# Softmax sums of short and last groups spread by VectorE instead of a DMA, longer planned DMA latencies, less forced filler

## The chip, the cores and the metric

One core of one Trainium2 chip. The metric is device time in microseconds (us), the median over executions. ACT is ScalarE, DVE is VectorE, PE is TensorE, POOL is GpSimd, SP is SyncE. One profile was taken of each kernel, so what is read from a profile carries the scatter of one execution; the slowest execution of a kernel in one series of runs lies 1 to 9 us above the fastest here.

## The reference, cut to what matters

```python
x = A_x                                    # [1, 2048, 512] bf16
x = x + _A_ref(_layernorm(x), A_wqkv, A_wo)
x = x + _B_ref(_layernorm(x), B_w1, B_w2)
x = x + _A_ref(_layernorm(x), A_wqkv, A_wo)
x = x + _B_ref(_layernorm(x), B_w1, B_w2)
# _A_ref: 32 heads of 16, softmax(q k^T / 4) v, then wo.   _B_ref: relu(h w1) w2, width 1792
```

Two layers, each attention and feed-forward. Attention has 2 x 32 x 2048 x 2048 exponentials. That is the work that matters; in this kernel ACT and DVE do it.

## The kernel before

The kernel plans its own order: while it is built, a small model with planned durations decides which instruction comes next on each engine. Each engine then runs its fixed order and waits on semaphores. A "slot" is one activation: three PSUM banks of scores (1536 columns). In about a quarter of the slots the third bank goes to DVE, which computes the exponential with integer and polynomial steps in pairs of banks, so ACT does 1024 columns. PE fills what is left of a slot with value matmuls, dense matmuls ("filler": projections and feed-forward) and, if nothing else fits, with repeated score matmuls, meant to keep its clock up.

The softmax sums of a group of 512 queries lie in one partition of each 32 of an accumulated tile `u`. To divide, the kernel gathers them into 128 partitions (`c`), takes the reciprocal, writes them back and spreads each row over 32 partitions (`r`) by a DMA:

```python
        def copy():
            ...                                        # u = sums and values out of PSUM
            if sg not in segs[-2:]:
                nc.sync.dma_start(out=c, in_=sums)     # the gather
                mark(("c", n), lag=3000.0)             # planned latency, ns
        def recip():
            nc.vector.reciprocal(out=c, in_=c)
            nc.sync.dma_start(out=sums, in_=c)         # the write-back
            nc.gpsimd.dma_start(out=r[:, 0:width], in_=...)   # the spread, [0, 32] repeated
            mark(("r", n), lag=9500.0)
        ...
            task(250, recip, [("r", n)], [("c", n)], place=0)
            task(180 + 1.1 * width, lambda: mul(0, width), ots + [("m", n)], [("r", n)] + war)
```

The last two groups of all take a shuffle on DVE instead, as nothing hides a DMA there. "Short groups" are those whose keys come in two or three parts; their partial sum is stored and loaded again (`sg["load"]`). Dense work is placed by pace, and is forced past the slot's limit when the pace is high:

```python
    def fill_pe(limit):
        while owed[0] > 0:
            limit_now = limit if owed[0] < 5.0 or not hurry[0] else now_pe[0] + 1000.0
            ...
        hurry[0] = pace > HURRY                        # HURRY = 2.0
    ...
    while pend:                                        # after the last slot
        emit_pv()
        run_dve(0.0, musts)
    run_all()                                          # whatever dense work is left, one PSUM bank
    wide[0] = True                                     # then the tail: last wo, layernorm, feed-forward
```

The softmax here doesn't subtract the row's maximum and nothing guards it: scores larger than these inputs give would overflow.

## Time and profile before

| Kernel before | us |
|---|---|
| median (3 runs) | 1757.56 (1755.46 to 1758.97) |
| span of the profiled execution | 1758.8 |
| start of the first exponential | 18.2 |
| end of the last exponential | 1726.5 |
| from there to the end ("the tail") | 32.3 |
| floor of ACT: slots by undisturbed start-to-start time | 1671.8 |
| loss: first start to last end, minus floor | 36.4 |

How to read it: three terms make the span. The prologue is load and layernorm; the tail is what must follow the last exponential; between them ACT sets the time, and what it does beyond its floor is a loss. How the floor is worked out from the start times of the activations, and why not from "idle", stands in the prediction, with the lines of the profile.

### The profile page before, as it was taken

How to read it: one execution, taken by the hardware profiler on the slowest of the kernel's cores; microseconds unless marked ns; L12 is line 12 of the kernel's file. 1: busy time of each engine (PE TensorE's matmuls, PEld its weight loads, DVE VectorE, ACT ScalarE, POOL GpSimd, SP SyncE). 2: the span in 40 equal slices, each digit the busy share in tenths (PEclk: the TensorE clock that was granted, in tenths of full speed). 3: DMA queues.
4: the chain of work that ended last, by engine and by line, in shares of the span. 5: the costliest groups of instructions: out<-in, count | busy, mean ns of one | idle time of the engine just before them, and what ended most of it. 6: DMA issues, size and time to landing. Idle time of an engine off the chain costs nothing.

```text
span 1758.8 us, 34642 instructions
## 1 busy us (share of the span) xinstructions
PE 1603.6 (91%) x14939; PEld 523.5 (30%) x15133; DVE 1482.0 (84%) x2221; ACT 1705.6 (97%) x1386; POOL 54.8 (3%) x105
## 2 busy tenths in 40 slices
PE   8898888999999999899899999879999999999998
PEld 2222222222222222222222222222222222444444
DVE  7438988888998999899789989879889888889884
ACT  6999999999999999999999999989999999999994
POOL 0000000000000000000000000000000000000000
PEclk9999999999999999999999999999999999999999
DMA  4001000110002000011000100010220021102112
GB/s 150 1 6 21 14 14 14 35 29 14 8 14 44 19 14 14 17 37 23 8 7 10 25 10 1 17 36 8 46 45 16 14 44 23 26 15 48 24 35 66
DMA packets 110937, 44.53 MB, mean 25 GB/s; under 512 B 98816, under 2 KB 106752, under 8 KB 110784
## 3 DMA queue, kind: packets, MB, share of 16 engines
q1 hardware_dynamic: 92192, 24.38, 6.0%
q0 software_dynamic: 17248, 16.63, 5.0%
q8 instruction: 118, 1.93, 0.4%
q10 hardware_dynamic: 1344, 1.31, 0.2%
q14 instruction: 35, 0.29, 0.1%
HBM read 22.54 MB, written 2.10 MB: 14 GB/s over the span
## 4 chain that ended last, share of the span: by engine, by line
ACT 84%; PE 11%; DVE 2%; issue 2%; DMA 1%; ACTq 0%
ACT e L1141 84%; PE ps_s L1132 4%; PE ps_o L823 3%; PE ps_f L409 2%; PE ps_s L1207 1%; DVE dy L900 0%; DMA c<-u 0%; DVE di L869 0%; DVE stats L438 0%; PE ps_f L1207 0%; PE ps_s L968 0%; DMA x<-in_A_x_dram 0%; DVE ht L622 0%; DVE q L570 0%; PE ps_s L477 0%
## 5 line engine op out<-in xcount | busy, mean ns | idle before, releaser
L1141 ACT ACTIVATE e<-ps_s 128x1536 bf16<-128x1536 f32 (+1 forms) x1366 | 1695.2, 1456 | 13.4 <-PE ps_s L1132 12.4
L1132 PE MATMUL ps_s<-q,ktp 32*128 32x512 bf16 (+1 forms) x7817 | 746.2, 357 | 118.6 <-ACT e L1141 91.3
L823 PE MATMUL ps_o<-e,vaug 128*32 128x512 bf16 (+1 forms) x4224 | 428.0, 363 | 4.7 <-DVE u L758 3.2
L1132 PEld LDWEIGHTS <-ktp 32*128 32x128 bf16 x7817 | 235.8, 92 | 619.3 <-issue 500.6
L869 DVE TENSOR_SCALAR di<-ps_s 128x512 int32<-128x512 f32 x338 | 232.3, 688 | 94.0 <-PE ps_s L1132 91.2
L823 PEld LDWEIGHTS <-vaug 128*32 128x32 bf16 x5376 | 144.9, 94 | 301.3 <-issue 277.6
L900 DVE SCALAR_TENSOR_TENSOR dy<-dm 128x1024 f32<-128x1024 f32 x169 | 206.4, 1221 | 3.8
L900 DVE SCALAR_TENSOR_TENSOR dy<-dy,dm 128x1024 f32<-128x1024 f32 x169 | 205.7, 1217 | 2.7
L900 DVE SCALAR_TENSOR_TENSOR de<-dy,di 128x1024 bf16<-128x1024 f32 x169 | 205.1, 1214 | 1.7
L894 DVE TENSOR_SCALAR dm<-di 128x1024 int32<-128x1024 int32 x169 | 116.6, 690 | 0.9
L823 PE MATMUL ps_o<-de,vaug 128*32 128x512 bf16 (+1 forms) x768 | 114.7, 358 | 2.2 <-DVE vaug L739 0.8
L894 DVE TENSOR_SCALAR di<-di 128x1024 int32<-128x1024 int32 x169 | 115.2, 681 | 1.7
L409 PE MATMUL ps_f<-xn2T,w 128*128 128x512 bf16 (+1 forms) x390 | 112.5, 368 | 4.4 <-issue 1.9
L409 PE MATMUL ps_f<-w,ht 128*128 128x512 bf16 x344 | 103.4, 383 | 4.5 <-issue 4.0
L783 POOL DMA_DIRECT2D r<-u x70 | 52.4, 748 | 1654.4 <-DMA u<-c 643.5
L622 DVE TENSOR_SCALAR ht<-ps_f 128x512 bf16<-128x512 f32 x105 | 72.1, 686 | 18.0 <-PE ps_f L409 15.9
L409 PE MATMUL ps_f<-xnT,wqkv 128*128 128x512 bf16 (+1 forms) x273 | 82.4, 372 | 3.4 <-issue 0.8
L570 DVE TENSOR_SCALAR q<-ps_f,qmask 128x512 bf16<-128x512 f32 (+1 forms) x94 | 63.1, 699 | 13.0 <-PE ps_f L409 11.4
L823 PE MATMUL ps_o<-di,vaug 128*32 128x512 bf16 (+1 forms) x384 | 70.9, 365 | 0.0
L409 PE MATMUL ps_f<-wo,ot 128*128 128x512 bf16 x207 | 63.5, 383 | 2.8 <-issue 2.2
L773 DVE SCALAR_TENSOR_TENSOR ot<-u,mask,r 128x512 bf16<-128x512 f32 (+2 forms) x74 | 49.8, 673 | 7.5 <-DMA r<-u 7.1
L409 PEld LDWEIGHTS <-w 128*128 128x128 bf16 x448 | 32.5, 97 | 73.1 <-issue 62.2
(85 smaller groups left out, 535.2 us busy)
## 6 DMA issues: line engine op xcount, KB each, us to landing
w<-in_B_w_dram SPq DMA_DIRECT2D x126, 128.0 KB
r<-u POOLq DMA_DIRECT2D x56, 256.0 KB, 7.1
out_dram<-x SPq DMA_DIRECT2D x16, 128.0 KB
x<-in_A_x_dram SPq DMA_DIRECT2D x14, 128.0 KB
w<-in_B_w_dram SPq DMA_DIRECT2D x1, 1792.0 KB
r<-u POOLq DMA_DIRECT2D x14, 128.0 KB, 4.6
wqkv<-in_A_wqkv_dram ACTq DMA_DIRECT2D x2, 512.0 KB
c<-u SPq DMA_DIRECT2D x56, 8.0 KB
```

The costliest lines, as they stand in the source:

```text
L409: nc.tensor.matmul(out, lhsT, rhs, start=i % k == 0, stop=i % k == k - 1)
L570: return nc.vector.tensor_scalar(out=qbuf[n % 2][e][:, 0:w], in0=b, scalar1=qmask[e][:, 0:1], scalar2=None, op0=ALU.mult,)
L622: nc.vector.tensor_scalar(out=htp[ft // 2][:, ft % 2 : ft % 2 + number, a : a + w], in0=b.rearrange("p (f q) -> p f q", f=number), scalar1 ...
L773: nc.vector.scalar_tensor_tensor(out=ot[t][:, at_column + a : at_column + a + w], in0=u[:, a : a + w], scalar=mask[e][:, 0:1], in1=r[:, a ...
L783: nc.gpsimd.dma_start(out=r[:, 0:width], in_=bass.AP(tensor=sums.tensor, offset=sums.offset, ap=[list(sums.ap[0]), [0, 32], [1, width]],),)
L823: nc.tensor.matmul(ps_o[32 * g : 32 * g + 32, 0 : sg["w"]], vaug[sg["l"]][kb][:, 4 * sg["T"] + g, 2 * e : 2 * e + 32], rhs, start=g not in ...
L869: first = nc.vector.tensor_scalar(out=di[:, half, :].bitcast(I32), in0=src, scalar1=EXP_BIAS, scalar2=0.0, op0=ALU.add, op1=ALU.max,)
L894: nc.vector.tensor_scalar(out=out[:].bitcast(I32), in0=di[:].bitcast(I32), scalar1=keep, scalar2=put, op0=ALU.bitwise_and, op1=ALU.bitwise_or,
L900: nc.vector.scalar_tensor_tensor(out=out[:], in0=x[:], scalar=c, in1=y[:], op0=ALU.add, op1=ALU.mult)
L1132: nc.tensor.matmul(b[:, a : a + sg["w"]], kt[32 * g : 32 * g + 32, kc : kc + P], qbuf[sg["n"] % 2][sg["e"]][32 * g : 32 * g + 32, 0 : sg[" ...
L1141: ex = nc.scalar.activation(out=eb[:, 0 : place[m]], in_=b[:, 0 : place[m]], func=ACTF.Exp, scale=1.0 / (LOG2E * UNIT),)
L1207: uses(nc.tensor.matmul(out, lhsT, rhs, start=first, stop=last), b, needs=needs)
```

## The change

The intent: no spread DMA where its latency stands in the way (short groups, last group of a chunk of queries); plan DMAs with the latency that they have, so that DVE does not block on one; and force less dense work between score matmuls, since that makes ACT wait.

```diff
-    HURRY = 2.0
+    C_LAG, R_LAG, U_LAG = 3600.0, 10500.0, 3000.0
...
+        quick = sg["load"] is not None or ended[l, j] == NT
...
         def recip():
             nc.vector.reciprocal(out=c, in_=c)
             nc.sync.dma_start(out=sums, in_=c)
-            nc.gpsimd.dma_start(
+            if not quick:
+                nc.gpsimd.dma_start(
...
-            mark(("r", n), lag=9500.0)
+            mark(("r", n), lag=U_LAG if quick else R_LAG)
+        def spread():
+            nc.vector.stream_shuffle(
+                out=r[:, 0:width], in_=u[:, 0:width], mask=[lane] * 32
+            )
+        def spread_mul():
+            if quick:
+                spread()
+            mul(0, width)
...
-            rest = sum(x[0][0]["early"] for x in itertools.islice(units, 400)) / W - 10.0
+            rest = sum(x[0][0]["early"] for x in itertools.islice(units, 400)) / W - 20.0
...
-        hurry[0] = pace > HURRY
+        hurry[0] = pace > (
+            2.0 if first["l"] and first["early"]
+            else 3.0 if not first["l"] and first["j"] == NQS - 1 else 99.0
+        )
```

Below, "the shuffle", "the lags" and "the filler rule" (the last two hunks) are its three parts.

More of the change, by code (lines that the diff above doesn't have):

```diff
@@ L765, in copy @@
                 nc.sync.dma_start(out=c, in_=sums)
-                mark(("c", n), lag=3000.0)
+                mark(("c", n), lag=C_LAG)
         musts.append((155 + 1.045 * width, now_pe[0] + PE_TO_DVE, copy))
@@ L778, in mul @@
                 mark(("ot", l, j, t, i))
+        ended[l, j] = ended.get((l, j), 0) + 1
+        quick = sg["load"] is not None or ended[l, j] == NT
         def recip():
@@ L782, in recip @@
             nc.sync.dma_start(out=sums, in_=c)
-            nc.gpsimd.dma_start(
-                out=r[:, 0:width],
-                in_=bass.AP(
-                    tensor=sums.tensor, offset=sums.offset,
-                    ap=[list(sums.ap[0]), [0, 32], [1, width]],
-                ),
-            )
-            mark(("r", n), lag=9500.0)
+            if not quick:
+                nc.gpsimd.dma_start(
+                    out=r[:, 0:width],
+                    in_=bass.AP(
+                        tensor=sums.tensor, offset=sums.offset,
+                        ap=[list(sums.ap[0]), [0, 32], [1, width]],
+                    ),
+                )
[3 more added lines that the diff above has]
+                out=r[:, 0:width], in_=u[:, 0:width], mask=[lane] * 32
+            )
+        def spread_mul():
+            if quick:
+                spread()
+            mul(0, width)
         def direct(i):
             if i == 0:
-                nc.vector.stream_shuffle(
-                    out=r[:, 0:width], in_=u[:, 0:width], mask=[lane] * 32
-                )
+                spread()
             a = i * P
@@ L811, in finish_segment @@
             task(250, recip, [("r", n)], [("c", n)], place=0)
-            task(180 + 1.1 * width, lambda: mul(0, width), ots + [("m", n)], [("r", n)] + war)
-        ended[l, j] = ended.get((l, j), 0) + 1
+            cost = 180 + 1.1 * width + (200 + 1.05 * width if quick else 0)
+            task(cost, spread_mul, ots + [("m", n)], [("r", n)] + war)
         if ended[l, j] == NT and not last:
```

## The prediction

> **What bounds the kernel now.** I read the page first (busy shares, chain), then the ScalarE (ACT) groups by shape, then the waits, then the timeline at two places where the chain leaves ACT.
>
> ```profile
> PE 1603.6 (91%) x14939; PEld 523.5 (30%) x15133; DVE 1482.0 (84%) x2221; ACT 1705.6 (97%) x1386; POOL 54.8 (3%) x105
> ...
> ACT 84%; PE 11%; DVE 2%; issue 2%; DMA 1%; ACTq 0%
> ```
>
> ACT is the bound: it computes the exponentials, and the chain that ended last is ACT for 84%. PE, 91% busy, is partly filler: score matmuls are repeated to keep it warm.
>
> ```profile
> L1141 ACT ACTIVATE e<-ps_s 128x1536 bf16<-128x1536 f32 x1027 | 1445.5, 1564 | 7.0 <-PE ps_s L1132 6.3
> L1141 ACT ACTIVATE e<-ps_s 128x1024 bf16<-128x1024 f32 x338 | 378.7, 1131 | 6.4 <-PE ps_s L1132 6.1
> ```
>
> Here the reader must not trust "idle": consecutive activations overlap, so a delay up to the overlap is counted as busy. I took start-to-start distances from the trace instead. Undisturbed, a 1536-wide one is followed after 1.330 us and a 1024-wide one (its third bank went to VectorE, DVE) after 0.903 us. 1027 x 1.330 + 338 x 0.903 + 0.68 for one 512-wide one = 1671.8 us. The stretch from the first start (18.2) to the last end (1726.5) is 1708.3 us. So the loop loses 36.4 us; 18.2 us of prologue and 32.3 us of tail make up the rest of the span.
>
> Where are the 36.4 us? Two kinds. First, waits on the DMAs that spread a group's softmax sums:
>
> ```profile
> ACT e L1141 <- PE ps_s L1132: 12.4, 28, 2.2
> ...
> DVE ot L773 <- DMA r<-u: 7.1, 9, 2.1
> ...
> DVE c L781 <- DMA c<-u: 4.6, 2, 3.3
> ```
>
> ```profile
> 1153.53 0.69 DVE L758 TENSOR_TENSOR u<-ktp,ps_o 128x512 f32<-128x512 f32 x1 [0.34 <-PE ps_o L823]
> ...
> 1160.57 0.25 DVE L781 RECIPROCAL c<-c 128x16 f32<-128x16 f32 x1 [3.30 <-DMA c<-u]
> ```
>
> ```profile
> 1165.00 1.02 ACT L1141 ACTIVATE e<-ps_s 128x1024 bf16<-128x1024 f32 x1 [2.17 <-PE ps_s L1132]
> 1166.58 1.45 ACT L1141 ACTIVATE e<-ps_s 128x1536 bf16<-128x1536 f32 x1 [0.55 <-PE ps_s L1132]
> ```
>
> Read downward: sums copied at 1153.5, DVE blocked for 3.30 us on the gather into c, all behind it late, ACT starved at 1165. Start-to-start, four slots from 1147 to 1167 lose 5.3 us. Three more delays with PE waiting for a late DVE copy lose 1.7 us, one at a clock drop (219 us) 1.4 us.
>
> Second, PE holding too much between two score groups ("forced filler"):
>
> ```profile
> 1256.96 1.02 ACT L1141 ACTIVATE e<-ps_s 128x1024 bf16<-128x1024 f32 x1 [0.18 <-PE ps_s L1132]
> 1258.36 1.02 ACT L1141 ACTIVATE e<-ps_s 128x1024 bf16<-128x1024 f32 x1 [0.37 <-PE ps_s L1132]
> ```
>
> 1.40 us from start to start instead of 0.90. In the program's order PE has there 5 value matmuls (1.67 passes, as three share the array), 2 dense and one score pass: 4.67 x 0.216 + 3 switches x 0.105 = 1.32 us against 0.90. I tallied every slot so: 32 are overloaded by over 0.3 us, and they lose 9.7 us. Small losses on the other slots make up the rest.
>
> **What the skill says.** "VectorE: DVE Perf Modes", section "The perf-mode tier table": the stream shuffle has only the 1x mode, about 2400 ns for 2048 elements. The trace agrees: its two shuffles of 256 took 438 ns, so a fixed 0.171 us beside 256/0.96 ns, and 512 elements should take 0.70 us (estimate). "DMA: Bandwidth & Descriptors", "Anatomy of one DMA — SWDGE (gpsimd) path" gives 2.0 us + bytes/436e3, 2.6 us for the 256 KB spread; the page's row for r<-u has 7.1 us to landing, and that decides. Same page, "Issuing engines are not separate DMA queues": all share 16 engines. This agrees with the gather from 1154: 6.0 us to its last packet against 1.5 usually, beside r transfers. "TensorE: Matmul & The Clock Gate", "What's actually happening": a window of 3413 ns with too little work halves PE's clock. The trace agrees: 3.4 us at 0.50 at 219.2, 1164.7 and 1738.1 us.
>
> **The change, part by part.**
>
> (a) Shuffle for the 20 groups with a carried partial sum and the last group of a chunk. The built programs give 70 spread DMAs before, 45 after; 2 shuffles before, 27 after (24 new of 512, one of 256). Removed per group: the wait from the written-back reciprocals to the landing, about 9.5 us from the reciprocal (2.4 to the issue, 7.1 in flight); left is a write-back of about 2 us and 0.70 us on DVE. DVE cost: 24 x 0.70 + 0.44 = 17.2 us. It saves the 5.3 us above and shortens chunk ends, where nothing waits visibly.
>
> (b) The longer lags (3.6 and 10.5 us planned for 3.0 and 9.5) let DVE's queue put other work first. They address the 11.7 us of DVE waits in the waits view; DVE is not the bound, so their worth is already in (a) and the small losses.
>
> (c) The built order has 166 DVE pairs instead of 169. A pair costs 2 x 0.688 + 1.221 + 1.217 + 1.214 + 0.690 + 0.681 = 6.40 us, so DVE gets 19.2 us back and stays even. ACT gets 6 banks more: 1033 x 1.330 + 332 x 0.903 + 0.68 = 1674.4, that is +2.6 us.
>
> (d) Less forced filler. The same tally on the new order: slots overloaded by over 0.3 us fall from 32 to 8. With the mean loss of each overload class from the trace (17 ns for slots with ample room, about 50 for mild ones, 350 for the worst) the old order gives 28.0 us and the new one 21.9. Saved: 6.1 us. Repeated score passes rise from 968 to 1033; they only fill holes.
>
> With (a) leaving perhaps 2 us of the 8.4 us DMA and late-copy losses, the loop loses 24 us instead of 36.4. With (c) its end comes 12.4 - 2.6 = 9.8 us earlier.
>
> (e) The price of (d), to be seen at the end of the order. The old order leaves half a feed-forward group of the last chunk but one (4 matmuls, one DVE evacuation) behind the last value matmuls; the new order leaves all seven (56 matmuls of 256 columns, 7 evacuations) there, through a single PSUM bank.
>
> ```profile
> 1725.47 1.42 PE L823 MATMUL ps_o<-e,vaug 128*32 128x256 bf16 x20
> ...
> 1726.83 0.61 PE L409 MATMUL ps_f<-xn2T,w 128*128 128x256 bf16 x4
> 1726.93 0.42 DVE L760 COPY u<-ps_o 128x256 f32<-128x256 f32 x1 [2.36 <-PE ps_o L823]
> ...
> 1727.48 0.69 DVE L622 TENSOR_SCALAR ht<-ps_f 128x512 bf16<-128x512 f32 x1
> ...
> 1728.09 0.43 DVE L794 STREAM_SHUFFLE r<-u 128x256 f32<-128x256 f32 x1
> ```
>
> With one bank, matmuls and evacuation alternate. 3, 5 and 6 matmuls took 0.50, 0.72 and 0.83 us elsewhere, so 8 take 1.04; with 0.04 to DVE, 0.69 and 0.06 back, a cycle is 1.83 us. Seven end 12.8 us after 1726.83; before, the shuffle of the last group started 1.26 us after it. Shift: +11.5 us, all exposed, as ACT is done and the last normalisation stands behind these evacuations. The weights are no limit: their last packet comes about 1.9 us after the issue, needed 3.7 us later. But PE is busy only 0.86 of 1.83 us, 47%; before the clock drop at 219 us I count 48%. A drop there doubles the matmul part for 3.4 us: +1 to +2.5 us.
>
> Sum: -9.8 + 11.5, plus 0 to 2.5, is +2 to +4 us. I shade this down to about 0, since my tally may underrate what falls away with the DMA traffic and late DVE work.
>
> **Rivals.** R1: the gain is real and the tail cheap, because the seven groups hide in waits that the tail has anyway: about 1746 us. For it: PE has idle time there. Against: order on both engines is fixed, and the group's chain (shuffle, reciprocals, product) stands behind the evacuations. R2: ACT stays where it was, as small losses take the place of the removed ones; then +2.6 +11.5 = 1772 us. For it: 17 us of shuffles sit in DVE's queue where PE waits for first steps and copies. Against: DVE's total is unchanged and its spread DMAs collide less. R3: DVE becomes the bound; 84% and unchanged speak against.
>
> **Range and chances.** The loop may gain 4 to 18 us, the tail may cost 9 to 15; most combinations lie between 1746 and 1767. Centre 1758 us. Faster by 2% needs under 1722.4 us, below the undisturbed loop with today's prologue and tail (18.2 + 1674.4 + 32.3 = 1724.9), so 1%. Slower by 2% needs 35 us of new loss, 1%. Within 2%: 98%.
>
> **What would show it.** Right: the last exponential ends at 1714 to 1719 us instead of 1726.5; from there to the end 43 to 47 us instead of 32.3, with seven evacuations 1.8 to 2.5 us apart; no 2 us ACT stall near 1150 to 1167; DVE waits on r and c near zero; 70 spread DMAs are 45; shuffles of 512 at 0.70 us. Wrong: a tail under 36 us (R1), or an exponential that ends near 1729 (R2).

## The result, and the profile after

| | before | changed |
|---|---|---|
| median, us (4 runs each) | 1757.47 | 1761.35 |
| range | 1755.46 to 1758.97 | 1759.60 to 1763.25 |
| ratio | | 1.0023 (1.0006 to 1.0040) |
| first exponential starts | 18.2 | 16.7 |
| floor of ACT | 1671.8 | 1674.4 |
| loss in the loop | 36.4 | 26.3 |
| tail | 32.3 | 42.0 |
| span of the profiled execution | 1758.8 | 1759.3 |

A ratio is the mean time of one kernel's fast runs over that of the other's of the same rounds, so it is not quite the ratio of the medians. The change is within 2%, and if anything slower. The terms moved by large amounts and cancel: start -1.5, floor +2.6, loss -10.1, tail +9.7, sum +0.7 against +0.5 between the spans (rounding). The start is scatter of the first loads: over all profiles it lies between 16.4 and 18.4 us. It is about half of why the two profiled spans are closer (+0.5) than the medians (+3.9): the profiled execution before was 3.1 us above its median, the changed one 0.3 below. The other half fits a clock drop: from the last shuffle to the end before took 30.7 us, with PE at half clock for 3.4 us from 1738.1, and the changed kernel 29.0 without one. Over all 14 profiles this stretch is 29.0 to 29.3 us in the nine without a whole drop in it, 30.7 in the four with one whole drop in it (before, e3, e7, e10) and 31.1 in e9. As e10 has the changed kernel's order there and has the drop, the 1.6 us belongs to the execution and not to the change. Without start and drop the terms give +2.6 - 10.1 + 11.3 = +3.8 us, which is what the medians show.

The changed kernel's page, busy shares and chain:

```profile
PE 1643.2 (93%) x15404; PEld 533.1 (30%) x15404; DVE 1481.9 (84%) x2250; ACT 1706.0 (97%) x1386; POOL 35.5 (2%) x80
...
ACT 82%; PE 12%; DVE 3%; issue 2%; DMA 1%; SPq 0%; ACTq 0%
```

ACT's total, 1706.0 us, is what it was, and so is DVE's. POOL lost a third with its spreads. Shares show nothing of the exchange; the chain hints at it, with DVE up from 2% to 3%. The ACT groups by shape give the counts behind the floor (L1156 is the line that was L1141):

```profile
L1156 ACT ACTIVATE e<-ps_s 128x1536 bf16<-128x1536 f32 x1033 | 1456.2, 1563 | 3.6 <-PE ps_s L1147 3.1
L1156 ACT ACTIVATE e<-ps_s 128x1024 bf16<-128x1024 f32 x332 | 374.5, 1136 | 1.8 <-PE ps_s L1147 1.7
```

The waits view has this row for ACT, and no row any more for DVE waiting on a spread into r or a gather into c (0.7 us for one write-back is left):

```profile
ACT e L1156 <- PE ps_s L1147: 4.8, 15, 0.6
```

The longest wait was 2.2 us and is 0.6. And this is the end of the changed kernel's timeline:

```profile
1716.85 0.87 PE L835 MATMUL ps_o<-e,vaug 128*32 128x256 bf16 x8 [0.43 <-ACT e L1156]
...
1717.65 1.05 PE L409 MATMUL ps_f<-xn2T,w 128*128 128x256 bf16 x8
...
1718.74 0.69 DVE L622 TENSOR_SCALAR ht<-ps_f 128x512 bf16<-128x512 f32 x1 [0.56 <-PE ps_f L409]
1719.48 1.03 PE L409 MATMUL ps_f<-xn2T,w 128*128 128x256 bf16 x8 [0.78 <-DVE ht L622]
...
1728.55 1.03 PE L409 MATMUL ps_f<-xn2T,w 128*128 128x256 bf16 x8 [0.78 <-DVE ht L622]
...
1729.62 0.69 DVE L622 TENSOR_SCALAR ht<-ps_f 128x512 bf16<-128x512 f32 x1 [1.12 <-PE ps_f L409]
...
1730.24 0.43 DVE L797 STREAM_SHUFFLE r<-u 128x256 f32<-128x256 f32 x1
...
1733.29 1.08 ACT L1232 CAST x<-ps_s 128x512 bf16<-128x512 f32 x2 [16.00 <-PE ps_s L1222]
```

Matmuls wait 0.78 us for the evacuation, the evacuation 1.12 us for the matmuls, seven times over, while ACT idles 16.0 us. The last normalisation (the shuffle at 1730.24) starts 12.6 us after the first of these matmuls; before it was 1.3.

### The profile page after: what moved, and what is told of

Same layout as the page of the kernel before. It is cut to its first block, busy times and chain, and to the rows that moved or that the text cites. A ratio compares the mean times of both kernels' runs of the same rounds, so it can differ in the third digit from the quotient of the medians.

```text
span 1759.3 us, 35344 instructions
## 1 busy us (share of the span) xinstructions
PE 1643.2 (93%) x15404; PEld 533.1 (30%) x15404; DVE 1481.9 (84%) x2250; ACT 1706.0 (97%) x1386; POOL 35.5 (2%) x80
## 4 chain that ended last, share of the span: by engine, by line
ACT 82%; PE 12%; DVE 3%; issue 2%; DMA 1%; SPq 0%; ACTq 0%
ACT e L1156 82%; PE ps_s L1147 4%; PE ps_f L409 4%; PE ps_o L835 3%; DVE dy L912 1%; PE ps_s L1222 1%; DVE ht L622 1%; DMA wqkv<-in_A_wqkv_dram 0%; DVE di L881 0%; DVE de L912 0%; DVE u L760 0%; PE ps_f L1222 0%; DMA x<-in_A_x_dram 0%; PE ps_s L980 0%; DVE stats L438 0%
## 5 line engine op out<-in xcount | busy, mean ns | idle before, releaser
L1156 ACT ACTIVATE e<-ps_s 128x1536 bf16<-128x1536 f32 (+1 forms) x1366 | 1695.6, 1458 | 5.4 <-PE ps_s L1147 4.8
L1147 PE MATMUL ps_s<-q,ktp 32*128 32x512 bf16 (+1 forms) x8100 | 761.5, 355 | 86.4 <-ACT e L1156 71.5
L1147 PEld LDWEIGHTS <-ktp 32*128 32x128 bf16 x8100 | 243.2, 92 | 605.9 <-issue 498.7
L881 DVE TENSOR_SCALAR di<-ps_s 128x512 int32<-128x512 f32 x332 | 228.1, 687 | 83.9 <-PE ps_s L1147 81.5
L912 DVE SCALAR_TENSOR_TENSOR dy<-dy,dm 128x1024 f32<-128x1024 f32 x166 | 201.8, 1216 | 2.0
L912 DVE SCALAR_TENSOR_TENSOR de<-dy,di 128x1024 bf16<-128x1024 f32 x166 | 201.2, 1212 | 1.1
L409 PE MATMUL ps_f<-xn2T,w 128*128 128x512 bf16 (+1 forms) x448 | 121.4, 370 | 4.7 <-DVE ht L622 4.7
L409 PE MATMUL ps_f<-w,ht 128*128 128x512 bf16 x392 | 113.9, 383 | 0.1
L409 PE MATMUL ps_f<-xnT,wqkv 128*128 128x512 bf16 (+1 forms) x312 | 91.5, 374 | 2.5 <-DVE ktp L530 1.2
L409 PE MATMUL ps_f<-wo,ot 128*128 128x512 bf16 x240 | 69.6, 383 | 1.0 <-DVE x L593 1.0
L787 POOL DMA_DIRECT2D r<-u x45 | 33.1, 736 | 1663.5 <-DVE di L881 558.8
```

The source lines that it names most:

```text
L409: nc.tensor.matmul(out, lhsT, rhs, start=i % k == 0, stop=i % k == k - 1)
L787: nc.gpsimd.dma_start(out=r[:, 0:width], in_=bass.AP(tensor=sums.tensor, offset=sums.offset, ap=[list(sums.ap[0]), [0, 32], [1, width]],),)
L881: first = nc.vector.tensor_scalar(out=di[:, half, :].bitcast(I32), in0=src, scalar1=EXP_BIAS, scalar2=0.0, op0=ALU.add, op1=ALU.max,)
L912: nc.vector.scalar_tensor_tensor(out=out[:], in0=x[:], scalar=c, in1=y[:], op0=ALU.add, op1=ALU.mult)
L1147: nc.tensor.matmul(b[:, a : a + sg["w"]], kt[32 * g : 32 * g + 32, kc : kc + P], qbuf[sg["n"] % 2][sg["e"]][32 * g : 32 * g + 32, 0 : sg[" ...
L1156: ex = nc.scalar.activation(out=eb[:, 0 : place[m]], in_=b[:, 0 : place[m]], func=ACTF.Exp, scale=1.0 / (LOG2E * UNIT),)
```

## The experiments

Each run is beside the kernel before on the same chip. "Short" is the loss in activations 870 to 1059, the short groups of layer 2 (about 1100 to 1340 us); "last" the loss in the last 150 activations. These, floor, loss and tail are worked out from one profile each, as above.

| run | median | ratio | floor | loss | short | last | tail |
|---|---|---|---|---|---|---|---|
| before | | | 1671.8 | 36.4 | 9.7 | 5.9 | 32.3 |
| changed | 1761.35 | 1.0023 | 1674.4 | 26.3 | 3.2 | 2.0 | 42.0 |
| e1 shuffle | 1763.32 | 1.0031 | 1671.0 | 43.9 | 16.8 | 8.3 | 30.2 |
| e2 lags | 1760.38 | 1.0014 | 1672.7 | 34.5 | 9.8 | 5.9 | 31.1 |
| e3 filler rule | 1768.81 | 1.0060 | 1675.2 | 35.2 | 10.8 | 3.3 | 43.7 |
| e4 changed, forced at the end | 1755.14 | 0.9981 | 1674.4 | 31.5 | 4.7 | 4.6 | 31.1 |
| e5 shuffle + lags | 1760.82 | 1.0016 | 1672.7 | 37.8 | 14.5 | 4.6 | 32.2 |
| e6 changed, 10 units | 1762.39 | 1.0022 | 1673.5 | 30.4 | 6.1 | 2.0 | 42.0 |
| e7 shuffle + filler rule | 1759.42 | 1.0001 | 1676.9 | 26.7 | 4.5 | 3.7 | 38.2 |
| e8 changed, three banks | 1761.41 | 1.0018 | 1674.4 | 26.4 | 3.3 | 2.0 | 40.6 |
| e9 lags + filler rule | 1775.59 | 1.0103 | 1673.5 | 29.2 | 5.8 | 5.2 | 54.9 |
| e10 changed, shuffles twice | 1765.61 | 1.0044 | 1674.4 | 29.2 | 4.4 | 2.0 | 43.6 |
| e11 e4 with 10 units | 1755.19 | 0.9988 | 1673.5 | 32.5 | 4.7 | 4.6 | 31.1 |
| e12 e4 with the old spread lag | 1752.13 | 0.9971 | 1673.5 | 29.5 | 3.8 | 5.3 | 30.2 |

All runs are within 2% of the kernel before. The 95% intervals of e5, e7 and e11 include 1. The scatter of one profile can be read off too: e4 and e8 run the changed kernel's order on ACT and DVE up to 1522 us, and lose 4.7 and 3.3 us in the short groups where it loses 3.2; e6 and e11 share an order there too, and lose 6.1 and 4.7. So figures of 3 to 5 us there cannot be told apart, while 9.7 and more stand clear of them.

The first theory, from the prediction: the filler rule and the shuffle save in the loop, the filler rule pays in the tail. The rival: the tail is hidden, and the loop's losses only moved.

### e1: the shuffle alone

```diff
 # changed kernel, with
-    C_LAG, R_LAG, U_LAG = 3600.0, 10500.0, 3000.0
+    C_LAG, R_LAG, U_LAG = 3000.0, 9500.0, 3000.0
+    HURRY = 2.0
...
+        hurry[0] = pace > HURRY        # and 10.0 for 20.0
```

> The kernel before with the shuffle alone (planned lags 3.0 and 9.5 us, forced filler as before). Theory (loop saves, tail pays): the built order has 340 two-bank slots (floor of ACT 0.8 us lower), 36 slots overloaded by over 0.3 us (tally 1.3 us worse), no spread DMA in the short groups (5.3 us of starved slots near 1147 to 1167 us gone), a tail with no more dense work than before: about 1752 us, tail about 32 us. Rival (the shuffle gives nothing, because its 17 us on DVE delay copies and first steps): 1757 us or more, with new waits of PE on DVE.

It missed: 1763.3, 0.31% slower than before, with 16.8 us lost in the short groups. The rival's number fits, and PE does wait for DVE, but e1's largest such wait (2.83 us) does not come from the shuffles' work: DVE itself stood for 3.73 us at a gather, as in the kernel before but at another place. Three queries of e1's timeline, in turn POOL, SP and DVE:

```profile
1284.12 0.68 POOL L788 DMA_DIRECT2D r<-u  x1 [25.94 <-DVE dy L913]
```

```profile
1284.42 0.56 SPq L766 DMA_DIRECT2D c<-u  x1
```

```profile
1291.25 0.25 DVE L785 RECIPROCAL c<-c 128x16 f32<-128x16 f32 x1 [3.73 <-DMA c<-u]
```

The gather was issued 0.30 us after the spread of an ordinary group. In the packets of this profile the spread's 4096 B packets run from 1285.4 to 1290.7, and the gather's 64 B packets do not begin before 1289.6. It took 6.5 us to its last packet; the median gather takes 1.5. The kernel before has one gather that slow, the 6.0 us one at 1154.2, 0.88 us behind a spread; four others there, 0.2 to 1.1 us behind a spread, took 1.5 to 1.9 us. What tells them apart is read off after e9. ACT then starved here, as its timeline shows:

```profile
1284.98 5.06 ACT L1154 ACTIVATE e<-ps_s 128x1536 bf16<-128x1536 f32 x4
1292.54 1.02 ACT L1154 ACTIVATE e<-ps_s 128x1024 bf16<-128x1024 f32 x1 [2.50 <-PE ps_s L1145]
```

So removing the spread from 25 groups does not remove the danger: an ordinary group just ahead of the short ones is enough. But the gather is a part of e1's loss only. DVE also waited 1.69 us (at 1132.8) and 2.50 us (at 1165.7) for late attention queries (the tile q), the stall that e5 shows below; the slots there lose 2.0 and 2.8 us, the slot at the gather 2.7.

### e2: the lags alone

```diff
-                mark(("c", n), lag=3000.0)
+                mark(("c", n), lag=3600.0)
...
-            mark(("r", n), lag=9500.0)
+            mark(("r", n), lag=10500.0)
```

> The kernel before with the longer planned lags alone. Theory: ACT's floor 0.9 us higher (336 two-bank slots), tally 1.6 us better, part of the DVE waits on c and r gone, worth perhaps 2 us, tail 0.5 us longer: 1755 to 1757 us. Rival (the lags are what helped the loop): 1752 us or less and no starved slots near 1150 us.

1760.4, 0.14% slower; a little above the expected range. In its profile the loss fell by 1.9 us, the floor rose by 0.9 and the short groups lost as much as before (9.8); but the profiled execution was e2's fastest, 3.4 us under its median, so the fall of the loss is not shown. A planned latency is not padding on one wait: it changes the built order, here by one DVE pair.

### e3: the filler rule alone

```diff
-        hurry[0] = pace > HURRY
+        hurry[0] = pace > (
+            2.0 if first["l"] and first["early"]
+            else 3.0 if not first["l"] and first["j"] == NQS - 1 else 99.0
+        )                              # and 20.0 for 10.0
```

> The kernel before with the changed rule for forced filler alone (and the 20 for 10 units in the pace of the short groups). Theory: ACT's floor 3.4 us higher (330 two-bank slots), overloaded slots 9 instead of 32 (5.2 us better), all seven feed-forward groups in the tail (9.7 us longer): about 1765 us, the slowest of the four. Rival (less forced filler is the gain and the tail is not its price): 1752 to 1756 us.

1768.8: the slowest of the first four, as the theory said, and further than it said. The tail is 43.7 us, 11.4 longer than before. In the last 150 slots the loss falls from 5.9 to 3.3. But the short groups lose 10.8 us, about half of it around a gather that a spread delayed to 6.8 us, with DVE blocked for 4.15 us. This profile is 3.6 us above e3's median.

### e4: the changed kernel, forced filler back at the very end

```diff
-            else 3.0 if not first["l"] and first["j"] == NQS - 1 else 99.0
+            else 3.0 if not first["l"] and first["j"] == NQS - 1
+            else 2.0 if first["l"] and first["j"] >= NQS - 1 else 99.0
```

> The changed kernel with forced filler allowed again in the last two half chunks of layer 2 only (pace over 2, as before the change). Theory: the tail gets back to 32 to 34 us, the last 150 slots lose about 2.6 us more: about 1755 us, 6 to 7 us under the changed kernel. Rival (the loop's loss only moved, the tail is hidden): 1761 us or more.

1755.1, as expected, 0.19% faster than the kernel before. Lines of e4's timeline:

```profile
1723.08 1.05 PE L409 MATMUL ps_f<-xn2T,w 128*128 128x256 bf16 x8
...
1724.16 0.69 DVE L622 TENSOR_SCALAR ht<-ps_f 128x512 bf16<-128x512 f32 x1 [0.55 <-PE ps_f L409]
...
1724.78 0.44 DVE L797 STREAM_SHUFFLE r<-u 128x256 f32<-128x256 f32 x1
```

One group is left behind the value matmuls instead of seven, and the last shuffle starts 1.7 us after it instead of 12.6. The price in the last 150 slots is 2.6 us (4.6 for 2.0), exactly the tally's figure; the gain in the tail is 10.9. (The loop's whole loss is 5.2 us higher, but the other 2.6 lie in slots whose order did not change, so they are scatter.) That settles the rival: the tail is exposed, and it ate the loop's gain.

### e5, e6, e7: which parts help the short groups

e1 and e3 lost more there than the whole change. A second theory: a gather issued just behind a spread blocks DVE, and shuffle and lags together end that. e5 is e1 with the new lags:

```diff
-    C_LAG, R_LAG, U_LAG = 3000.0, 9500.0, 3000.0
+    C_LAG, R_LAG, U_LAG = 3600.0, 10500.0, 3000.0
```

> Shuffle and longer lags, forced filler as before. In the earlier runs the loop's differences lie in the short groups of layer 2 (1100 to 1310 us: 9.7 us lost before, 3.2 changed, 16.8 with the shuffle alone, 10.8 with the filler rule alone). Theory (a gather of sums that is issued within about 2 us after a 256 KB spread takes 5 to 7 us and blocks VectorE; shuffle and lags together end that): loss there under 5 us, last 150 slots about 6 us, tail about 31 us, in all 1750 to 1754 us. Rival (the built order of the short groups, set by the 20 for 10 units, is what helps): loss there 9 us or more, 1758 us or more.

It missed: 14.5 us lost, 1760.8 in all. One gather again took 6.5 us, 0.40 us behind a spread, and DVE waited 3.1 us. Two more stalls have nothing to do with a DMA. Lines of e5's timeline at one of them:

```profile
1130.48 0.39 PE L410 MATMUL ps_f<-xnT,wqkv 128*128 128x512 bf16 x1
1130.91 1.41 DVE L571 TENSOR_SCALAR q<-ps_f,qmask 128x512 bf16<-128x512 f32 x2 [2.37 <-PE ps_f L410]
1131.72 0.39 PE L1145 MATMUL ps_s<-q,ktp 32*128 32x512 bf16 x2 [0.85 <-DVE q L571]
...
1132.99 2.37 ACT L1154 ACTIVATE e<-ps_s 128x1024 bf16<-128x1024 f32 x2 [1.17 <-PE ps_s L1145]
```

The queries of the next group were projected too late: the last of their matmuls ended at 1130.9, DVE had waited 2.37 us for it, PE waits 0.85 us for DVE, ACT for PE. In short groups new queries are needed about every 14 us (in the trace before, DVE has them at 1148.1 and 1162.6), so there is little room for a late one.

e6 is the changed kernel with 10 units in the pace:

```diff
-            rest = sum(x[0][0]["early"] for x in itertools.islice(units, 400)) / W - 20.0
+            rest = sum(x[0][0]["early"] for x in itertools.islice(units, 400)) / W - 10.0
```

> The changed kernel with 10 units again in the pace of the short groups of layer 2. Theory (gather behind spread): loss from 1100 to 1310 us stays under 5 us, ACT's floor 0.9 us lower, tail 42 us: about 1760 us. Rival (the 20 units make the order that helps): loss there 9 us or more, 1766 us or more.

6.1 us lost, between the two answers; 1762.4. The 20 units may be worth up to 3 us, but one profile each does not settle that. No gather was slow.

e7 is the changed kernel with the old lags:

```diff
-    C_LAG, R_LAG, U_LAG = 3600.0, 10500.0, 3000.0
+    C_LAG, R_LAG, U_LAG = 3000.0, 9500.0, 3000.0
```

> The changed kernel with the old planned lags (3.0 and 9.5 us). ACT's floor is 2.5 us higher (326 two-bank slots), and three of the seven feed-forward groups are back inside the loop, so the tail is about 5.5 us shorter. Theory: without the longer lags VectorE meets late gathers again, loss from 1100 to 1310 us 6 to 10 us: about 1761 us. Rival (lags don't matter there): loss 3 us, about 1758 us.

4.5 us lost and 1759.4: between the theory's figures and the rival's. One gather took 5.9 us behind a spread and DVE waited 2.2 us, but the order around it had slack. Three of the seven groups were back in the loop, as the count of the order said, and the tail is 38.2.

### e8: three PSUM banks for the work behind the last slot

```diff
+    tail_banks[0] = [ps_f[:], ps_s[0][:, 0, :], ps_s[1][:, 0, :]]   # bank() takes these in turn
     run_all()
+    tail_banks[0] = None
```

> The changed kernel with three PSUM banks in turn instead of one for the feed-forward groups behind the last value matmuls; the loop is untouched. Theory (the single bank makes matmuls and evacuation alternate at 1.81 us): the cycle falls to about 1.5 us, where the reload of the weight buffers (ready 2.95 us after the group that frees them began) bounds it, so the tail is about 2 us shorter, 1759 us. Rival (the bank isn't the limit): cycle 1.8 us, 1761 us.

The median, 1761.4, did not move. In the trace the mechanism is as expected: from the first of these matmuls to the last shuffle 11.2 us instead of 12.6, tail 40.6 instead of 42.0. This execution began its exponentials 1.7 us later than the changed kernel's, which hides that in its span, and 1.4 us is below what five rounds resolve. Lines of its timeline:

```profile
1722.54 0.61 PE L414 MATMUL ps_s<-xn2T,w 128*128 128x256 bf16 x4 [1.07 <-DMA w<-in_B_w_dram]
1723.48 0.81 PEld L414 LDWEIGHTS <-w 128*128 128x128 bf16 x8 [0.61 <-DMA w<-in_B_w_dram]
1723.48 0.61 PE L414 MATMUL ps_s<-xn2T,w 128*128 128x256 bf16 x4 [0.34 <-DMA w<-in_B_w_dram]
```

With the bank free, PE waits for weights: the reload of the four weight buffers takes the bank's place as the limit.

### e9: lags and filler rule, no shuffle

```diff
 # e3, with
-                mark(("c", n), lag=3000.0)
+                mark(("c", n), lag=3600.0)
-            mark(("r", n), lag=9500.0)
+            mark(("r", n), lag=10500.0)
```

> Longer lags and the filler rule, without the shuffle. So far the loss in the short groups of layer 2 was 9.7 us before, 16.8 with the shuffle alone, 14.5 with shuffle and lags, 10.8 with the filler rule alone, 4.5 with shuffle and filler rule, 3.2 with all. Theory (it takes the shuffle and the filler rule together; either alone gives nothing there): loss there 9 us or more, all seven groups in the tail (42 us), about 1767 us. Rival (filler rule and lags suffice, the shuffle is beside the point): loss there under 5 us, about 1762 us.

This completes the eight combinations of the three parts. The theory was wrong: the short groups lost 5.8 us without the shuffle. So did it miss the time, 1775.6, by the tail: 54.9 us. Here even the layernorm ahead of the seven groups fell behind the last slot, PE idled 2.6 us for it, and its clock went to half at 1722.8 and stayed there for 23.9 us. Lines of e9's timeline, and its busy time by stretch (us of the stretch, then each engine's busy time; the last three columns are clock, DMA share and GB/s):

```profile
1726.79 0.69 DVE L622 TENSOR_SCALAR ht<-ps_f 128x512 bf16<-128x512 f32 x1 [1.96 <-PE ps_f L409]
1729.44 0.69 DVE L622 TENSOR_SCALAR ht<-ps_f 128x512 bf16<-128x512 f32 x1 [1.96 <-PE ps_f L409]
1732.08 0.69 DVE L622 TENSOR_SCALAR ht<-ps_f 128x512 bf16<-128x512 f32 x1 [1.95 <-PE ps_f L409]
```

```profile
1725.00:1744.00 19.00, 14.31 (x60) 8.42 (x59) 5.45 (x10) 0.00 (x0) 0.00 (x0) 0.50 0.40 91
```

The cycle is 2.65 us at half clock instead of 1.81. Over seven cycles that is 5.9 us; the prediction allowed 0 to 2.5 us for it.

Over the eight combinations, the short groups lose 9.7, 16.8, 9.8 and 14.5 us with the old filler rule, and 10.8, 4.5, 5.8 and 3.2 with the new one. So the filler rule goes with the gain there, once it has one of the others beside it; the shuffle alone made it worse. The name misleads here, as the code shows: while layer 2's groups store partial sums (894 to 1112 us in the changed kernel) the threshold is still 2.0 and the 20 units raise the pace, which makes forcing likelier there and not rarer; only after that, in the short groups, is nothing forced.

The gathers over 5 us were one each in the kernel before, e1, e2, e5, e7 and e9 and two in e3; there was none in the changed kernel, e4, e6, e8 and e10 to e12. A tally over the 14 traces shows which gathers they are. Number the spreads of a kernel in order of issue. Eight gathers were issued up to 2 us behind the first, fifth, ninth ... spread: seven took 5.3 to 6.5 us. (The eighth, in e9, took 1.6: its packets began before the spread's.) Ten were issued as close behind the other spreads: all took 1.5 to 2.5 us. The eighth slow gather, in e3, was issued together with such a fourth-in-turn spread. The write-backs from c agree: within 5 us behind the first, fifth, ninth ... spread 14 took 2.7 to 5.6 us, behind the others 21 took 1.7 to 2.1. So here only every fourth spread does harm. In the changed kernel the one gather near such a spread was issued 0.35 us ahead of it (at 1280.1) and took 1.5 us; in e1, e5 and e7 it was issued 0.3 to 1.2 us behind. This was read from the traces and not tested by a run.

### e10: the shuffles twice

```diff
             if quick:
                 spread()
+                spread()
             mul(0, width)
```

> The changed kernel with every new shuffle run twice (same result, same planned order): about 17 us more work on VectorE. Theory (VectorE has room, the shuffles lie beside ACT's work): at most 3 us slower than the changed kernel, up to 1764 us. Rival (the shuffles delay copies and first steps that PE waits for, so their cost is on the path): 8 us or more slower, 1769 us.

1765.6, 4.3 us above the changed kernel's median, between the two answers; the intervals of the two ratios overlap (1.0031 to 1.0056, 1.0006 to 1.0040). DVE did 17 us more (1499.0 busy instead of 1481.9); the loop's loss rose by 2.9 us, and the tail by 1.6, which is the clock drop at 1742.9 that the changed kernel's profile did not have. So the shuffles are not on the path: at most about a sixth of an added microsecond reaches the loop's end, and 2.9 us is hardly more than the scatter of one profile. The first 25 shuffles need not cost what 25 more do.

### e11 and e12: to beat both

```diff
 # e4, with (e11)
-            rest = ... / W - 20.0
+            rest = ... / W - 10.0
 # e4, with (e12)
-    C_LAG, R_LAG, U_LAG = 3600.0, 10500.0, 3000.0
+    C_LAG, R_LAG, U_LAG = 3600.0, 9500.0, 3000.0
```

> A candidate to beat both: the changed kernel with forced filler in the last two half chunks and 10 units again in the pace of the short groups. ACT's floor 0.9 us lower than in the run with the end alone (334 two-bank slots), the loss in the short groups perhaps 1.5 us higher: about 1755 us.

> A second candidate: the changed kernel with forced filler in the last two half chunks and the spread planned with 9.5 us as before. ACT's floor 0.9 us lower than in the run with the end alone (334 two-bank slots), two fewer overloaded-slot gains (tally 0.4 us worse), nothing of the dense work left behind the last value matmuls (tail 1 us shorter): about 1754 us.

e11: 1755.2, as expected. e12: 1752.1, 0.29% below the kernel before (interval 0.9958 to 0.9983) and the best of all, 1.9 us better than expected. It has nothing left behind the last value matmuls (tail 30.2), a loss of 29.5, and 0.9 us less floor than e4. Both beat the changed kernel; e12 clearly beats both.

## Why the prediction was right or wrong

The measured 1761.35 lies in the range, and the class (within 2%) was the likely one. Point by point, by its own steps:

- **The bound.** Right. ACT's floor and losses plus the tail make the time in every run of the table.
- **(a) The shuffle.** The counts and cost were right: 45 spreads, 27 shuffles, 0.72 us measured for 512 elements where 0.70 was estimated. The saving in the short groups was 6.5 us (9.7 to 3.2) where 5.3 was said. The reason given was wrong: the shuffle does not earn it. Alone it costs 7 us there (e1), and filler rule and lags get to 5.8 without it (e9). The prediction saw that the slow gather ran beside spreads, but not that a spread which the change keeps can do the same. And its 5.3 us are not all the gather's: 1.5 of them were lost in the slot from 1147.3, 7 us before that gather was issued. There PE waited for a late tile q, as in e5:

```profile
1149.52 1.02 PE L1132 MATMUL ps_s<-q,ktp 32*128 32x512 bf16 x10 [1.18 <-DVE q L570]
```

- **(b) The lags.** "Their worth is already in (a)" fell. DVE's waits on r and c went to zero in the changed kernel, but the lags alone leave one slow gather and 9.8 us in the short groups (e2). Their effect cannot be told from that of the order they produce.
- **(c) ACT's floor.** Right: +2.6 us, by counts.
- **(d) Less forced filler.** The size, 6.1 us, is not shown. The last 150 slots fell by 3.9 us (e4 gives back 2.6 of it when forcing returns), slots 200 to 839 only from 13.0 to 12.0, and the first 200 rose from 3.8 to 5.7. The larger part of the effect is in the short groups, where the rule changes which work stands when; alone (e3) it took 1.2 us off the whole loss. The prediction's counts of repeated score passes, 968 and 1033, are not those of the traces (about 1240 and 1334: 7817 and 8100 score matmuls, three to a pass, less one pass for each of 1366 slots); nothing rests on them.
- **The loop.** Loss 26.3 for the 24 said; the last exponential ended 9.2 us earlier for the 9.8 said, of which 1.5 us is the earlier start.
- **(e) The tail.** Right, and the heart of it: seven evacuations 1.81 us apart (1.83 said), the last shuffle 11.3 us later relative to the value matmuls (11.5 said). The added clock drop did not come in the changed kernel's profile, and the one at 1738 is not in it; from the last shuffle to the end it was 29.0 us instead of 30.7. So the tail grew by 9.7 net. That last 1.6 us is the execution's, as e10 shows, and not a gain of the change. In e9 the drop came, and cost more than allowed.
- **What would show it.** The last exponential ended at 1717.3 (1714 to 1719 said); the tail, 42.0, fell just under the 43 to 47 said, for want of that drop (e10, with it: 43.6).
- **The sum.** +2 to +4 us was worked out, +3.9 measured. The shading down to 0, "since my tally may underrate what falls away with the DMA traffic and late DVE work", is the step that failed: nothing more fell away. That the sum fits so well is partly luck: it counted up to 2.5 us for a clock drop that did not come, and the loop's loss fell by 10.1 us for the 12.4 worked out; the two misses cancel. The likely range, 21 us wide, would have held most outcomes. R1's 1746 and both ends of that range lie about 2 us lower than the prediction's own terms give (1757.6 - 9.8 = 1747.8).
- **Rivals.** R1 (the tail is hidden) was excluded by the trace and by e4, R2 (small losses take the place) by the loss of 26.3. R3 did not occur. Doubled shuffles (e10) leave R2 a small core at most.

What stays open: why the filler rule helps in the short groups. Orders differ everywhere at once. Late queries are one mechanism that was seen: PE waited for them in the short groups in the kernel before (1.18 us), e1, e2, e5 (0.85 each) and e3 (0.75), and in no run with the new filler rule and one of the other parts. No run changed this alone, so it is not shown to be the whole.

## What to carry to other kernels

When work is no longer forced into the bound's stretch, look at the end of the built order for where it went: each piece left behind the last instruction of the bounding engine costs its full latency chain there. Here six groups more cost 10.9 us of tail, where forcing them into the loop cost 2.6. A planned latency or a pace in a scheduler is not an isolated knob; changing it rewrites the order everywhere, so test parts in all combinations before crediting one. And when a small DMA is late, look at which large DMA was issued just before it, before shortening its own path; look also at the cases in which the same neighbour did no harm, since here only every fourth one did.

## What the Trainium skill lacked or had wrong

- "DMA: Bandwidth & Descriptors", "Anatomy of one DMA — SWDGE (gpsimd) path": 2.0 us + bytes/436e3 makes 2.6 us for the 256 KB spread; its landing took 7.1 us (median of 56 before and of 32 after). The formula alone misleads here, but the page does not lack the reason: under "Why a DMA increments its semaphore by 16 and not by 1" it says that the slowest dimension of an access pattern limits how many of the 16 engines a transfer uses. The spread's source has four partitions there. In e1's trace of one spread 19.9 us of packets went through in 5.3 us, so about four at a time.
- The same page, "Issuing engines are not separate DMA queues", says that transfers of different engines interleave. In e1 an 8 KB gather issued 0.30 us behind a spread put through its first packet 5.2 us later, when the spread was nearly done (6.5 us instead of 1.5). Eight such gathers (5.3 to 6.8 us) were seen in twelve runs and the kernel before. The page lacks how late a small transfer can come behind a large one. Which ones are hit it lets one guess: by the section on the semaphore, a transfer from the sync engine takes the lowest-numbered engines and one from gpsimd the next ones in turn. Four of 16 in turn would be the same four at every fourth spread, as in the tally after e9. The traces do not name the engines, so this is argued, not shown.
- "TensorE: Matmul & The Clock Gate", "What's actually happening", gives the window (3413 ns; here drops of 3.4 us or multiples) but not how much work in it keeps the clock. In the changed kernel PE was busy 5.17 of 9.07 us (57%) from 1719.48 to 1728.55, five of the seven cycles, and kept full clock; in e9 the clock stayed at half for 23.9 us with PE busy 14.31 of 19.00 us (75%) at that half clock.
- "VectorE: DVE Perf Modes", "The perf-mode tier table": the shuffle's 1x rate held (0.44 us for 256 elements, 0.72 for 512). Nothing was lacking here.
